# A recurrent attention with two dense layers: the order of all five engines taken from a list scheduler in the kernel's source

## The chip, the core and the metric

The kernel runs on one core of a Trainium2 chip. The core has five engines with a queue each: PE (TensorE) multiplies matrices, DVE (VectorE), ACT (ScalarE) and POOL (GpSimd) work element by element, and SP (SyncE) issues the DMA transfers. Each engine works through its own instructions in the order in which the program lists them, and semaphores hold an instruction back until its inputs are there. The metric is the device time of one execution in microseconds (us); the median of three runs stands for a kernel.

## The reference, cut to what matters

```python
batch, n_heads, seq, head_dim = 4, 8, 768, 40
for t in range(S):                                  # attention: a state per head, step by step
    y[:, :, t] = einsum('bhd,bhde->bhe', rt, state)
    Sa = einsum('bhde,bhe->bhd', state, at)
    state = state * wt - einsum('bhd,bhe->bhde', Sa, bt) + einsum('bhd,bhe->bhde', vt, kt)
x = y as (3072 tokens, 320)
h = x @ w_in                                        # layer one: 320 -> 2048 -> 320
x = (h * sigmoid(1.702 * h)) @ w_out
g, val = x @ w_gate, x @ w_val                      # layer two: 320 -> 1536 -> 320
out = (silu(g) * val) @ moe2_w_out
```

All weights arrive in 64 bits and are converted to 32 in the kernel.

## The kernel before, in words

The attention is worked out in chunks: 12 steps of 64 tokens (`T`, `NT`), all 32 heads at once. A step has two halves. The first half does not depend on the state. It loads the step's data (`load_w`, `load_a`, `load_kb`, `load_v`, `load_r`, `load_vt`, all issued by SP), forms the running products of the decays forward and backward (`scan`, `rec`, L371 and L386, on DVE), scales the keys with them (`scale_kb`, `scale_a`, L392 and L396), and multiplies keys by keys on PE (`g_nb`, L411 to L414, into the tile nb through ACT, L415; `g_nk`, L427). nb holds a triangular system. Its 32 by 32 blocks are inverted column by column in `solve`: DVE transposes nb to nsol (L448), 31 pivots follow, each a product (L462, tmp) and an addition (L467, tsol) that depend on each other, and a transposition gives tt (L471). The pivots of a step stand on fixed engines: the first 16 on DVE, the last 15 on POOL. Two small products (`g_q`, L487; `g_t`, L504) complete the inverse.

The second half carries the state mt from step to step: `g_w` (L523, L535), `g_u` (L558), `g_ut` (L575), `g_m` (L594), two score products `g_s` (L621), the result `g_y` (L639, L661) and the transposed state `g_mt` (L609). Its result goes by six small DMAs to the tile xm (`x_move`) and is split into a high and a low part in xst (`x_split`, L690 to L695), the input of layer one.

Layer one (`Up`) takes 512 tokens at a time, so two attention steps feed one of its six blocks m. For each of 16 slices f of the hidden layer, `h_part` issues 8 matmuls of 512 columns (L222), ACT applies Silu and copies the high part (L226, L228), POOL subtracts to get the low part (L230, gl), and `o_part` issues 8 matmuls two slices later (L244 to L253). The block of step pair (2m, 2m+1) can start when both steps are split. Layer two (`Down`) follows when layer one is done; it is not changed.

What sets the order around the change: in `layer_one` PE's order is the source's (`manual_schedule` with PE alone): 16 slots i a step, in each at most one or two attention products and then 8 matmuls of layer one, taken from the generator `dense`. Within a step, `g_w` stands in slot 0, `g_nb` of the next step in slot 1, `g_nk` and `g_y` in slot 8, `g_mt` in slot 9, `g_tok` in slots 10 and 11, `g_q` in slot 13, `g_t` in slot 15. The order of DVE, ACT, POOL and SP comes from the framework's scheduler, with priorities shifted by `later(att.tc, -200)` for pivots and `later(att.tc, 300)` for conversions. The weights' conversion (`Convert`, three operations on DVE, two on ACT and one on POOL for a piece, 89 pieces) is spread over the steps by `spread_out`: the 44 pieces of layer one over the first 3.5 steps, the 45 of layer two after them. The attention products share two PSUM tiles of two banks each; layer one's h product has one bank. nb, nsol, tsol, tt, q and kb exist once; a and c twice.

```python
engines = (nc.vector, nc.vector) if n == 0 else (nc.gpsimd, nc.vector)
init, work, end = att.solve(engines)
...
if i == 13 and ahead:
    att.g_q()
```

Of the kernel before, what the change touches and what calls it, by code (L numbers as in the profile page):

```python
# [20 lines left out]
T = 64  # L21
# [13 lines left out]
class later:  # L35
    def __init__(self, tc, off):
        self.tc, self.off = tc, off

    def __enter__(self):
        self.tc.cur_priority += self.off  # L40

    def __exit__(self, *a):
        self.tc.cur_priority -= self.off


# [12 lines left out]


TINY = 3.4332275390625e-05  # L60


class Convert:
# [4 lines left out]
    def __init__(self, tc, ctx):  # L68
        self.tc = tc
        self.nc = tc.nc  # L70
        self.p = ctx.enter_context(tc.tile_pool(name="cv", bufs=1))
        self.ps = Ring(ctx, tc, "cvs", 2)
        self.p2 = Ring(ctx, tc, "cv2", 2)
        self.p3 = Ring(ctx, tc, "cv3", 3)
        self.p1 = Ring(ctx, tc, "cv1", 1)

    def piece(self, src, finish):

        nc = self.nc
        st = {}  # L80
        wide = src.dtype != F32
        rows, cw = src.shape[0], src.shape[1] // (2 if wide else 1)

        def take():
            st["w"] = self.p2.tile([128, self.CW], F32, tag="cvw", name="cvw")

        def load():
            if wide:
                a = st["a"] = self.p3.tile([128, self.CW, 2], U32, tag="cva", name="cva")
                nc.sync.dma_start(out=a[0:rows, 0:cw].rearrange("p c k -> p (c k)"), in_=src)  # L90
            else:
                take()
                nc.sync.dma_start(out=st["w"][0:rows, 0:cw], in_=src)

        def square():
            take()
            lo, hi = (st["a"][0:rows, 0:cw, k] for k in range(2))
            nc.scalar.activation(out=st["w"][0:rows, 0:cw], in_=hi.bitcast(F32), func=ACTF.Square)  # L98

            nc.scalar.activation(out=lo, in_=lo, func=ACTF.Copy, scale=2.0 ** -29)  # L100

        def step(i):
            v = nc.vector
            lo, hi = (st["a"][0:rows, 0:cw, k] for k in range(2))
            if i == 0:
                st["u"] = self.p1.tile([128, self.CW], U32, tag="cvu", name="cvu")
            u, w = (st[n][0:rows, 0:cw] for n in "uw")
            f = u.bitcast(F32)
            if i == 0:
                v.tensor_scalar(  # L110
                    out=u, in0=hi, scalar1=3, scalar2=0x3FFFFFF8, op0=ALU.logical_shift_left, op1=ALU.bitwise_and
                )
            if i == 1:
                v.scalar_tensor_tensor(
                    out=u, in0=hi, scalar=0xC0000000, in1=u, op0=ALU.bitwise_and, op1=ALU.bitwise_or
                )
            if i == 2:
                v.scalar_tensor_tensor(out=f, in0=w, scalar=TINY * TINY, in1=f, op0=ALU.is_ge, op1=ALU.mult)  # L118
            if i == 3:
                nc.gpsimd.tensor_tensor(w.bitcast(U32), u, lo, op=ALU.add)  # L120

        steps = [square] + [lambda i=i: step(i) for i in range(4)] if wide else []
        return load, steps, lambda: finish(st["w"][0:rows, 0:cw])

    def split_out(self, w, view, *dst):

        nc = self.nc
        t = view(self.ps.tile([128, 512], F32R, tag="cvs", name="cvs"))
        hi, lo = t[:, 0], t[:, 1]
        w = w.rearrange("p (a c) -> p a c", c=hi.shape[2])  # L130
        nc.scalar.activation(out=hi, in_=w, func=ACTF.Copy)
        nc.gpsimd.tensor_tensor(lo, w, hi.bitcast(F32), op=ALU.subtract)
        n = hi.shape[1] // len(dst)
        for i, d in enumerate(dst):
            nc.sync.dma_start(out=d, in_=t[:, :, n * i:n * i + n].rearrange("p h a c -> p a h c").bitcast(F32))

    @staticmethod
    def chain(pieces):

        out = [pieces[0][0]] + [None] * 4  # L140
        finish = None
        for i, (_, steps, f) in enumerate(pieces):
            if finish and not steps:
                out.append(finish)
                finish = None
            if i + 1 < len(pieces):
                out.append(pieces[i + 1][0])
            out += steps[:3]
            if finish:
                out.append(finish)  # L150
            out += steps[3:]
            finish = f
        return out + [None, None, finish]


class Up:
# [9 lines left out]
    def __init__(self, tc, ctx, cst, w_out, x2s, side):  # L166
        self.nc, self.cst, self.w_out, self.x2s = tc.nc, cst, w_out, x2s
        pool = lambda name, bufs, **kw: Ring(ctx, tc, name, bufs, **kw)
        self.wp = pool("f_w", 1, side=side).pool
        self.xp = pool("f_x", 2, side=side)  # L170
        self.sp = pool("f_s", 3, side=side)
        self.gp = pool("f_g", 3, side=side)
        self.ph = pool("f_ph", 1, space=PSUM)
        self.pa = pool("f_pa", 1, space=PSUM)
# [99 lines left out]
    def steps(self):  # L274
# [12 lines left out]
        for x in lag:  # L287
            yield from self.o_part(*x)
# [1003 lines left out]
```

## Time and profile before

| | us |
|---|---|
| median of three runs | 1485.36 (1475.73 to 1490.98) |
| the profiled execution, device time | 1484.43 |
| its span, first to last instruction | 1482.6 |
| DVE busy, ACT busy, POOL busy | 658.5, 437.4, 393.9 |
| PE busy | 1161.4 |

The page of a profile gives busy times of engines, the chain of work that ended last, and the costliest groups of instructions. The views behind it ask the same execution for the busy time in stretches, for the instructions of one source line, for the engines' waits and for the instructions in order of time. A number such as x768 is a count; a name such as nsol<-nb reads "writes nsol, reads nb".

### The profile page before, as it was taken

To read this page: it belongs to the slowest core of one execution; us is meant where nothing else is said; L and a number is where in the kernel's file an instruction comes from. 1 tells how busy PE (TensorE), PEld (TensorE's weight loads), DVE (VectorE), ACT (ScalarE), POOL (GpSimd) and SP (SyncE) were. 2 spreads that over 40 slices of the span, in tenths; PEclk is the share of its full clock that TensorE was granted. 3 is DMA by queue.
4 is the path that set the end of the run, shared out by engine and by line. 5 is a ranking of instruction groups with operands and counts; after the bars stand their busy time and mean duration, and the time that the engine had idled before them with its cause. 6 is when DMAs were issued, how large, how long until landed. Compare 5 with 4: busy or idle time off the path is not lost.

```text
span 1482.6 us, 38220 instructions
## 1 busy us (share of the span) xinstructions
PE 1161.4 (78%) x16897; PEld 973.8 (66%) x16897; DVE 658.5 (44%) x1197; ACT 437.4 (30%) x830; POOL 393.9 (27%) x544
## 2 busy tenths in 40 slices
PE   1353449286877968687777788698999999999998
PEld 1353437265666857566666667586778888888887
DVE  5576575445645455525455463323433232323222
ACT  2123243233333223122323232324532222222221
POOL 3014453646444242414343443221000000000000
PEclk9975559678897879778988979799999999999999
DMA  6116151444525252323525252324620010100000
GB/s 153 49 55 190 50 165 56 135 119 119 148 87 153 71 164 85 120 80 109 149 67 144 67 159 77 111 63 160 214 63 22 19 39 1 39 1 19 1 18 20
DMA packets 71240, 131.99 MB, mean 89 GB/s; under 512 B 7128, under 2 KB 27608, under 8 KB 71064
## 3 DMA queue, kind: packets, MB, share of 16 engines
q1 hardware_dynamic: 71064, 129.45, 29.5%
q8 instruction: 134, 2.20, 0.6%
q14 instruction: 42, 0.34, 0.1%
HBM read 103.08 MB, written 19.79 MB: 83 GB/s over the span
## 4 chain that ended last, share of the span: by engine, by line
PE 50%; DVE 16%; POOL 12%; DMA 10%; issue 8%; ACT 2%; SPq 1%; POOLq 0%; DVEq 0%; ACTq 0%
PE gv L931 18%; PE h L222 6%; DVE tsol L467 4%; POOL tmp L462 4%; POOL tsol L467 4%; DVE tmp L462 3%; PE oacc L951 3%; PE oacc L952 3%; PE oacc L953 3%; POOL cvw L120 3%; DMA kb<-kba 3%; PE psw L535 2%; PE acc L249 2%; PE psw L523 2%; PE acc L251 2%
## 5 line engine op out<-in xcount | busy, mean ns | idle before, releaser
L931 PE MATMUL gv<-xst,wg 128*128 128x512 f32 x1152 | 281.5, 396 | 1.8 <-ACT sg L934 1.8
L931 PEld LDWEIGHTS gv<-xst,wg 128*128 128x128 f32 x1152 | 214.2, 188 | 48.7 <-ACT sg L934 2.3
L222 PE MATMUL h<-xst,wi 120*128 120x512 f32 x768 | 214.8, 423 | 18.8 <-ACT sg L226 15.6
L222 PEld LDWEIGHTS h<-xst,wi 120*128 120x128 f32 x768 | 148.1, 200 | 56.7 <-ACT sg L226 18.1
L230 POOL TENSOR_TENSOR gl<-sg,gh 128x512 fp32r<-128x512 f32 x82 | 117.4, 1432 | 222.7 <-ACT gh L228 210.9
L935 DVE TENSOR_TENSOR sg<-gv,sg 128x512 f32<-128x512 f32 x72 | 49.8, 691 | 230.0 <-PE gv L931 230.0
L120 POOL TENSOR_TENSOR cvw<-cvu,cva 128x256 uint32<-128x256 uint32 (+2 forms) x89 | 72.4, 814 | 175.0 <-DVE cvu L118 132.7
L249 PE MATMUL acc<-gh,wo 128*128 128x512 f32 x192 | 91.3, 476 | 5.8 <-DMA wo<-w_out 3.2
L609 PE MATMUL psd<-cst,mt 104*104 104x104 f32 x96 | 18.8, 375 | 91.0 <-DVE su L667 91.0
L952 PE MATMUL oacc<-wo,zh 128*128 128x320 f32 x288 | 88.9, 309 | 0.0
L951 PE MATMUL oacc<-wo,zh 128*128 128x320 f32 x288 | 88.8, 309 | 0.0
L953 PE MATMUL oacc<-wo,zl 128*128 128x320 f32 x288 | 88.3, 309 | 0.0
L934 ACT ACTIVATE sg<-gv 128x512 f32<-128x512 f32 x72 | 43.1, 599 | 151.0 <-PE gv L931 151.0
L427 PE MATMUL psk<-a,kb 40*64 40x64 f32 x768 | 22.6, 299 | 83.0 <-DVE su L624 62.6
L226 ACT ACTIVATE sg<-h 128x512 f32<-128x512 f32 x96 | 56.5, 588 | 97.9 <-PE h L222 92.3
L251 PE MATMUL acc<-gh,wo 128*128 128x512 f32 x192 | 84.0, 438 | 0.0
L253 PE MATMUL acc<-gl,wo 128*128 128x512 f32 x192 | 83.5, 436 | 0.0
L98 ACT ACTIVATE cvw<-cva 128x256 f32<-128x256 f32 (+2 forms) x89 | 38.1, 431 | 148.7 <-DMA w_gv<-cvw 83.7
L937 ACT ACTIVATE zh<-sg 128x512 fp32r<-128x512 f32 x72 | 45.5, 631 | 123.0 <-DVE sg L935 123.0
L110 DVE TENSOR_SCALAR cvu<-cva 128x256 uint32<-128x256 uint32 (+2 forms) x89 | 40.8, 459 | 90.3 <-POOL cvw L120 82.0
L609 PEld LDWEIGHTS psd<-cst,mt 104*104 104x104 f32 x96 | 14.9, 197 | 95.5 <-DVE su L667 95.4
L427 PEld LDWEIGHTS psk<-a,kb 40*64 40x64 f32 x768 | 20.4, 206 | 84.7 <-DVE su L624 63.7
(126 smaller groups left out, 2199.9 us busy)
## 6 DMA issues: line engine op xcount, KB each, us to landing
wo<-w_out SPq DMA_DIRECT2D x48, 640.0 KB
kb<-kba SPq DMA_DIRECT2D x24, 416.0 KB
cva<-out SPq DMA_DIRECT2D x35, 256.0 KB
cva<-gv SPq DMA_DIRECT2D x30, 256.0 KB
xm<-su SPq DMA_DIRECT2D x72, 80.0 KB
wdec<-wd SPq DMA_DIRECT2D x12, 422.9 KB
a<-kba SPq DMA_DIRECT2D x12, 416.0 KB
r<-rT SPq DMA_DIRECT2D x12, 416.0 KB
```

The source lines that it names most:

```text
L120: nc.gpsimd.tensor_tensor(w.bitcast(U32), u, lo, op=ALU.add)
L222: nc.tensor.matmul(ps, self.wi[:, b, 128 * f:128 * f + 128], x[:, a], start=(i == 0), stop=(i == 7))
L230: self.sub.tensor_tensor(lo, sg, hi.bitcast(F32), op=ALU.subtract)
L249: nc.tensor.matmul(acc[i], w[:, c:c + 128], hi, start=st, stop=False)
L251: nc.tensor.matmul(acc[i], w[:, 256 + c:384 + c], hi, start=False, stop=False)
L253: nc.tensor.matmul(acc[i], w[:, c:c + 128], lo, start=False, stop=sp)
L462: eng.tensor_tensor(tv, tsol[:, o:16, u:u + 1].to_broadcast([128, n, u]), nsol[:, u:u + 1, 0:u].to_broadcast([128, n, u]), op=ALU.mult,)
L467: eng.tensor_tensor(t, t, tv, op=ALU.add)
L931: nc.tensor.matmul(ps, w[:, b], x[:, a], start=(i == 0), stop=(i == 7))
L951: nc.tensor.matmul(acc[k], hi[:, c], self.wo[:, f, 0], start=st, stop=False)
L952: nc.tensor.matmul(acc[k], hi[:, c], self.wo[:, f, 1], start=False, stop=False)
L953: nc.tensor.matmul(acc[k], lo[:, c], self.wo[:, f, 0], start=False, stop=sp)
```

## The change

Every operation up to the end of the attention becomes a task with an engine (or a choice of engines), a cost in microseconds written in the source, the names it reads and writes, and a due value. `Plan.order` runs a list scheduler over all tasks while the kernel is built: it takes the task that can begin first and, among those of the same engine that can begin within 0.12 us of it, the one with the smallest due value. The resulting order is the program order of all five engines (`manual_schedule()` with no list of engines). A group of 8 matmuls of layer one is one PE task with the largest due value, so it goes where no attention product can begin. Tasks that may run on DVE or POOL are given to the one that would finish first: the pivots (product and addition of one pivot on one engine), the scaling of a and of both halves of kb, layer one's low part gl, and the low part in the split of xm. All copies of q and of tt out of PSUM go to ACT (half of them were on DVE). nb has two buffers. The two PSUM tiles are handed out by the plan. Tiles that rotated through rings become fixed tiles with the same numbers of buffers. `y_part(1)` no longer stands ahead of the rest of `g_y`, `g_m` stands ahead of `g_ut`, the last step leaves out `g_m`, and md is cleared once on POOL. Layer one's operations that the plan begins after the attention's last operation run after it under the framework's scheduler, as before, there with a second PSUM bank for h; four jobs of layer two's weights are issued after each PE task of it, instead of one after each matmul. The number of DMAs and their sizes stay, their order on SP is the plan's.

The diff, cut to its core:

```diff
+class Plan:
+    SEM, RATE, LATENCY, SLACK = 0.15, 215.0, 2.0, 0.12
...
+    def order(self):
+        free, ready, done = {}, {}, []
+        sets = [0.0] * self.sets
+        wire = 0.0
...
+        def start(t, e):
+            s = max(t.est[e], free.get(e, 0.0))
+            if t.bank and t.bank.slot is None:
+                if min(sets) >= 1e9:
+                    return None
+                s = max(s, min(sets))
+            mine = s + t.choice[e]
+            for o, c in t.choice.items():
+                if o != e and max(t.est[o], free.get(o, 0.0)) + c < mine - 1e-9:
+                    return None
+            return s
...
+            now, _, _, e, _ = min(found, key=lambda x: x[:3])
+            now, _, _, e, t = min((x for x in found if x[3] == e and x[0] <= now + self.SLACK),
+                                  key=lambda x: (x[1], x[2]))
...
+            if t.kb:
+                wire = max(wire, t.end) + t.kb / self.RATE
+                t.end = wire + self.LATENCY
...
 class Up:
...
+        def pe(cost, fn, reads, writes):
+            last[0] = add("PE", cost, fn, reads, writes, after=(last[0],))
+            last[0].due = 1e6
...
+            pe(1.95, mm, [f"x{m % 2}.{y}" for y in range(2)] + w, ("h",))
+            add("ACT", 0.6, silu, ("h",), (f"sg{s}",))
+            add("ACT", 0.63, lambda: nc.scalar.activation(out=hi, in_=sg, func=ACTF.Copy), (f"sg{s}",), (f"gh{d}",))
+            add(("POOL", "DVE"), (1.43, 0.69), lambda e: self.engine(e).tensor_tensor(lo, sg, hi.bitcast(F32), op=ALU.subtract),
+                (f"sg{s}", f"gh{d}"), (f"gl{d}",))
...
 class Attention:
...
-        self.nb = one.tile([128, 16, T], F32, name="nb")
+        self.nb = [one.tile([128, 16, T], F32, name=f"nb{i}") for i in range(2)]
...
+        nc.gpsimd.memset(self.md, 0.0)
...
+        plan.add("DVE", 2.4, scan, ("wdec",), (ck,), due + 0.1)
+        plan.add("DVE", 3.35, back, ("wdec",), ("rc",), due + 0.12)
+        plan.add(("POOL", "DVE"), (2.3, 1.7), scale_a, (ck,), (ak,), due + 0.13)
+        plan.add(("DVE", "POOL"), (1.7, 2.3), lambda e: scale(1, e), ("rc",), ("kb1",), due + 0.14)
...
+        plan.add("DVE", 2.0, turn, (nbk,), ("nsol",), due + 0.1)
+        for u in range(31, 0, -1):
+            x = (16 - u // 2) * u
+            both, cost = ("DVE", "POOL"), (0.2 + 0.0008 * x, 0.22 + 0.0019 * x)
+            t = plan.add(both, cost, lambda e, u=u: product(e, u), ("nsol", "tsol"), ("tmp",), due + 0.1)
+            plan.add(both, cost, lambda e, u=u: update(e, u), ("tmp",), ("tsol",), due + 0.1, same=t)
...
+        plan.add("PE", 1.15, q_mm, (nbk, "tt1"), ("q.p",), due + 0.84, bank=bq, into=("q0", "q1"))
+            plan.add(("ACT",), (0.75,), lambda e, p=p: move(e, bq, p, self.q), ("q.p",), (f"q{p}",), due + 0.85, bank=bq)
...
+        plan.add("PE", 2.4, w_mm, (ak, "mt", "nk", "v"), ("w.p",), due, bank=bw, into=("w",))
+        plan.add(("ACT",), (0.75,), w_out, ("w.p",), ("w",), due, bank=bw)
...
 def layer_one(att, up, conv, first, second):
...
+    dense = up.tasks(plan)
+    next(dense)
     for n in range(NT):
+        att.prepare(plan, n, n - 1.0)
+        if n == 1:
+            for q in range(4):
+                convert(first[q], 0.2 if q == 0 else 1.4 + 0.5 * q, 0.05)
+        if n > 3:
+            i = len(second) * (n - 4) // 8
+            convert(second[i:len(second) * (n - 3) // 8], n - 0.9, 0.15)
+        att.advance(plan, n, n)
+        if n % 2:
+            next(dense, None)
+    order = plan.order()
+    end = max(t.begin for t in order if not hasattr(t, "dense"))
+    with att.tc.manual_schedule():
+        for t in order:
+            if t.begin <= end:
+                t.run()
+    return [t for t in order if t.begin > end]
...
+                    up.tail = True
+                    for t in tail:
+                        t.run()
+                        if t.eng == "PE":
+                            down.prepare(4)
```

## Rows read from the trace of the kernel before

**Rows 1.** The page: its span, and the busy time of each engine.

```profile
span 1482.6 us, 38220 instructions
...
PE 1161.4 (78%) x16897; PEld 973.8 (66%) x16897; DVE 658.5 (44%) x1197; ACT 437.4 (30%) x830; POOL 393.9 (27%) x544
```

**Rows 2.** Busy us (instructions) of each engine by stage, granted PE clock, DMA share, GB/s.

```profile
0.00:1005.00 1005.00, 697.95 (x14604) 577.34 (x14605) 511.92 (x965) 297.54 (x580) 388.78 (x540) 0.81 0.37 109
1005.00:1077.00 72.00, 66.56 (x280) 52.89 (x279) 30.20 (x58) 37.62 (x78) 5.15 (x4) 0.98 0.58 188
1077.00:1470.00 393.00, 391.19 (x1980) 338.17 (x1979) 114.14 (x172) 100.85 (x171) 0.00 (x0) 1.00 0.07 21
...
0.00:144.00 144.00, 52.18 (x1548) 48.28 (x1552) 93.42 (x206) 34.89 (x71) 40.43 (x38) 0.82 0.41 113
```

**Rows 3.** Line L558: shortest, median, longest ns; its first and last start, us.

```profile
L558 PE MATMUL psu<-w,tt x768: 225/226/326, 76.3 to 977.7; 64*64 64x40 f32 x192
```

**Rows 4.** Chain of work that ended last, one step: start us, us, what.

```profile
570.26 1.13 PE psw L535 x32
...
576.03 1.04 ACT nb L415
577.09 1.99 DVE nsol L448
...
605.01 1.06 DVE tt L471
```

**Rows 5.** Instructions of PE in order of time, the same step: start us, us.

```profile
633.66 1.20 PE L487 MATMUL psq<-tt,nb 32*32 32x32 f32 x64
...
642.51 1.74 PE L504 MATMUL psx<-q,tn 32*32 32x32 f32 x62 [0.48 <-DVE q L494]
...
647.89 1.40 PE L523 MATMUL psw<-mt,a 40*64 40x40 f32 x22
```

**Rows 6.** Waits of all engines, 0 to 1003 us: us in total, times, longest.

```profile
DVE nsol L448 <- ACT nb L415: 118.0, 11, 18.4
...
DVE tt L471 <- POOL tsol L467: 80.3, 10, 11.8
```

**Rows 7.** Instructions of POOL and of DVE in order of time, around 556 us.

```profile
556.10 1.28 POOL L230 TENSOR_TENSOR gl<-sg,gh 128x512 fp32r<-128x512 f32 x1
```

**Rows 8.** The same of DVE.

```profile
556.14 2.32 DVE L392 TENSOR_TENSOR kb<-kb,rc 104x1024 f32<-104x1024 f32 x1 [5.95 <-DMA kb<-kba]
```

**Rows 9.** Single lines: count, shortest/median/longest ns, first and last start us.

```profile
L386 DVE TENSOR_TENSOR_SCAN rc<-wdec,rc x12: 2302/4029/4035, 9.6 to 871.2; 104x1040 f32<-104x1040 f32 x12
...
L392 DVE TENSOR_TENSOR kb<-kb,rc x12: 1215/1702/3007, 12.0 to 881.8; 104x1024 f32<-104x1024 f32 x12
...
L392 POOL TENSOR_TENSOR kb<-kb,rc x12: 2178/2198/3156, 13.9 to 879.3; 104x1024 f32<-104x1024 f32 x12
...
L230 POOL TENSOR_TENSOR gl<-sg,gh x82: 1260/1280/2859, 221.7 to 1024.1; 128x512 fp32r<-128x512 f32 x82
...
L230 DVE TENSOR_TENSOR gl<-sg,gh x14: 673/692/694, 1027.6 to 1073.3; 128x512 fp32r<-128x512 f32 x14
...
L462 DVE TENSOR_TENSOR tmp<-tsol,nsol x222: 178/264/1292, 35.3 to 912.3; 128x126 f32<-128x126 f32 x13, 128x31 f32<-128x31 f32 x11, 128x58 f32<-128x58 f32 x11, 128x81 f32<-128x81 f32 x11
L462 POOL TENSOR_TENSOR tmp<-tsol,nsol x150: 217/366/1217, 167.1 to 928.6; 128x135 f32<-128x135 f32 x10, 128x126 f32<-128x126 f32 x10, 128x130 f32<-128x130 f32 x10, 128x120 f32<-128x120 f32 x10
...
L118 DVE SCALAR_TENSOR_TENSOR cvu<-cvw,cvu x89: 353/425/1479, 23.1 to 992.7; 128x256 f32<-128x256 f32 x65, 120x256 f32<-120x256 f32 x16, 80x256 f32<-80x256 f32 x8
...
L120 POOL TENSOR_TENSOR cvw<-cvu,cva x89: 722/732/3402, 23.7 to 993.2; 128x256 uint32<-128x256 uint32 x65, 120x256 uint32<-120x256 uint32 x16, 80x256 uint32<-80x256 uint32 x8
```

**Rows 10.** Single lines of the first step and the copies, as in rows 9.

```profile
L411 PE MATMUL psn<-a,kb x768: 212/238/313, 15.1 to 900.0; 40*32 40x64 f32 x192
...
L448 DVE STREAM_TRANSPOSE nsol<-nb x12: 1901/1966/1985, 33.3 to 901.6; 128x1024 f32<-128x1024 f32 x12
...
L509 DVE COPY tt<-psx x12: 689/689/691, 65.9 to 966.8; 32x512 f32<-32x512 f32 x12
```

More of the change, by code (lines that the diff above doesn't have):

```diff
@@ new lines, in piece @@
+        self.count += 1
+        wk = f"cvw{i % 2}"
+        w = self.w[i % 2][0:rows, 0:cw]
+        if not wide:
+            load = lambda: nc.sync.dma_start(out=w, in_=src)
+            return [("SP", 0.5, load, (), (wk,), rows * cw / 256)] + finish(w)
+        ak = f"cva{i % 3}"
+        a = self.a[i % 3]
+        lo, hi = (a[0:rows, 0:cw, k] for k in range(2))
+        u = self.u[0:rows, 0:cw]
+        f = u.bitcast(F32)
+        def load():
+            nc.sync.dma_start(out=a[0:rows, 0:cw].rearrange("p c k -> p (c k)"), in_=src)
@@ L95, in square, with low @@
         def square():
-            take()
-            lo, hi = (st["a"][0:rows, 0:cw, k] for k in range(2))
-            nc.scalar.activation(out=st["w"][0:rows, 0:cw], in_=hi.bitcast(F32), func=ACTF.Square)
+            nc.scalar.activation(out=w, in_=hi.bitcast(F32), func=ACTF.Square)
+        def low():
             nc.scalar.activation(out=lo, in_=lo, func=ACTF.Copy, scale=2.0 ** -29)
[L102 to L120, printed above, removed]
@@ L137, in chain, with put @@
[L137 to L153, printed above, removed]
+        def put(j, d):
+            nc.sync.dma_start(out=d, in_=t[:, :, n * j:n * j + n].rearrange("p h a c -> p a h c").bitcast(F32))
@@ L199, in set_m, with copy @@
         hi, lo = self.wi[0:80, 4, c], self.wi[0:80, 5, c]
[L200 to L202 removed]
+        def copy(t):
             nc.sync.dma_start(
@@ L433, in g_tok @@
[L433 to L447 removed]
+        a, c, kb = self.a[n % 2], self.c[n % 2], self.kb
@@ new lines, in prepare @@
+        for p in range(2):
+            plan.add(("ACT",), (0.75,), lambda e, p=p: move(e, bt, p, tt[:, :, 32:64]), ("t.p",),
+                     ("tt0",) if p else ("tt0.0", "tt0"), due + 0.87, bank=bt)
+        plan.add(("POOL", "DVE"), (2.3, 1.7), lambda e: scale(0, e), ("rc",), ("kb0",), due + 0.3)
+        for k in range(2):
+            self.tokens(plan, k, due + 0.5 + 0.1 * k)
+        load(self.v.rearrange("q i d -> q (i d)"), self.vtok[n], "v", 328, 0.6)
+        load(self.r.rearrange("q p h t -> q (p h t)"), self.rT[n], "r", 416, 0.65)
@@ new lines, in give @@
+        k1 = tuple(f"xm1.{i}" for i in range(3, 6))
+        for i in range(4):
+            o = 2 * i if i < 2 else i + 2
+            keys = k0 if i < 2 else k1
+            f = (lambda e, i=i: low(e, i)) if i < 2 else (lambda e, o=o: mixed(o))
+            plan.add("ACT", 0.43, lambda o=o, i=i: high(o, i), keys, (f"xp{i}",), due, into=(key,))
+            es, cs = (("DVE", "POOL"), (0.62, 1.4)) if i < 2 else (("DVE",), (0.62,))
+            plan.add(es, cs, f, keys + (f"xp{i}",), (f"xq{i}",), due)
@@ L700, in bad_flag @@
+        plan.add("NONE", 0.001, lambda: None, tuple(f"xq{i}" for i in range(4)), (key,), due)
 def bad_flag(nc, tc, att, bad):
@@ new lines, in layer_one, with convert @@
+def layer_one(att, up, conv, first, second):
+    nc = att.nc
+    plan = Plan(2)
+    def convert(jobs, due, step):
+        for i, job in enumerate(jobs):
+            for eng, cost, fn, reads, writes, kb in job():
+                plan.add(eng, cost, fn, reads, writes, due + step * i, kb=kb)
+    dense = up.tasks(plan)
+    next(dense)
+    for n in range(NT):
+        att.prepare(plan, n, n - 1.0)
[15 more added lines that the diff above has]
+    return [t for t in order if t.begin > end]
```

1111 lines of the change are left out of this document (553 added, 558 removed).

## The prediction

> **What bounds the kernel now.** I read the page first. PE is busy for 1161.4 of 1482.6 us, but no engine is near full over the whole span [rows 1]. So I cut the span into stages [rows 2]. From 1077 to 1470 us layer two keeps PE busy for 391.2 of 393 us at full clock: that stage is PE's, and the change leaves it alone. From 1005 to 1077 us the last block of layer one runs, PE busy 66.6 of 72 us. The first 1005 us hold the attention and five of the six blocks. There PE is busy 698 us at a mean granted clock of 0.81, DVE 512, POOL 389, ACT 298: nobody is full. Something other than an engine's work sets that stage, and it holds two thirds of the time.
>
> The line of the u product shows the pace, since its 64 matmuls come once a step: the first at 76.3 us, the last step's at about 977.7 us [rows 3]. That is 901.4 us for 11 steps, 81.9 us each.
>
> The chain of waits shows what one step is made of [rows 4]. The w product of step 6 ends at 571.4, nb is out of PSUM at 577.1, nsol ready at 579.1, and the pivots run to 605.0, where tt starts. The inverse is needed next by psq on PE, which starts at 633.7 [rows 5]: 28 us after tt. The source puts psq in slot 13, behind the key products, y, the transposed state and the tokens, and PE works in that order whatever is ready. psx follows at 642.5 and the next w product at 647.9. So of 81 us, 26 are pivots, 28 are order, 14 the rest of the inverse, and the rest is w and nb. The waits say the same at the other end: DVE spends 118.0 us in 11 waits, 10.7 each, on nb, whose product stands behind the w product; and 80.3 us in ten waits on the POOL half of the pivots [rows 6].
>
> **The change part by part.** The sum is total = S + 11 x T + R, with S the start of the first u product, T the pace and R what follows the last one. Now it is 76.3 + 11 x 81.9 + 504.9 = 1482.6; the profiled device time is 1484.4, 1.8 more, and the median of the runs, 1485.4, is 0.9 above that.
>
> R, 504.9 us, is taken as unchanged. It holds the last 28 us of attention, block six, and layer two. Layer two's weight jobs now come 4 for a group of 8 matmuls instead of 8. There are 108, so they take 27 of the 32 groups. DVE and ACT, which do them, are busy 30 and 38 of those 72 us [rows 2], which hides it; without that cover at most the 5 last groups' worth, 5 x 72/32 = 11 us, would be late.
>
> S: the first key product starts at 15.1 us, nsol only at 33.3 [rows 10], while in the later step [rows 4] nsol starts 5.7 us after the w product's end. With 5 us from psn to nsol the inverse moves up by about 13 us, to S = 63; some of the order behind the pivots falls as well. I take 55, with 50 to 76 as bounds.
>
> T is the question. Three things bound it once the order is free.
>
> First the pivots. nsol, tsol and tt exist once, so a step cannot be shorter than its 62 dependent operations and a transposition: 26 us in rows 4. That is far below 81.9, so the ring of the inverse doesn't bind. The second nb belongs here: it lets the next nb be written while psq still reads the old one. Its cost is memory alone.
>
> Second PE. In 1005 us it has 698 us of work at clock 0.81 [rows 2]. If all of that shrinks with the clock it is 565 us at full clock. A step thus needs between 565/12 = 47 and 698/12 = 58 us, with layer one's groups (five blocks) in it.
>
> Third the pair of DVE and POOL, to which the change gives shared tasks. One case shows how it behaves: a gl on POOL from 556.10 to 557.38 [rows 7], and a key scaling on DVE that starts at 556.14 and takes 2.32 us [rows 8], where the shortest takes 1.22 [rows 9]: 1.10 longer, nearly all of gl's 1.28. The backward product takes 2.30 us at its shortest and 4.03 in the median. So two operations of these forms run one after the other even on two engines. The Trainium skill, page "SBUF — State Buffer", section "Who interferes with whom", says that a DVE instruction with two SBUF inputs and a GpSimd one that reads SBUF exclude each other and that the later one is blocked until the first ends. The row agrees. It speaks against sharing.
>
> I add up that work at undisturbed durations [rows 9]. Fixed: conversion on DVE 89 x 3 x 0.425 = 113, on POOL 89 x 0.73 and 44 split subtractions taken as equal, 97; two products of decays a step, 24 x 2.30 = 55. Shared: 744 pivot operations x 0.264 = 196 on DVE, x 0.366 = 272 on POOL; 80 gl x 0.69 = 55 or x 1.28 = 102; 36 scalings x 1.22 = 44 or x 2.20 = 79. All shared on DVE 265 + 295 = 560 us, all on POOL 265 + 453 = 718. A step is 47 to 60 us of exclusive work, 53 at half. The other end is that nothing of DVE and POOL overlaps and today's waits stay in: (511.9 + 388.8)/12 = 75 us. Transpositions and reads of PSUM on DVE are in the 75 and need not exclude POOL.
>
> I take T = 61. It is above the middle of the exclusive work, 53, because operations in a fixed order are late whenever one of another engine is, and above PE's 58 at today's clock; it is nearer to 53 than to 75 because the 75 counts blocked time twice. The gain of 20.9 us a step is less than the 28 + 10.7 us of order found above, so it has room there.
>
> The other edits cost little. Twenty-four copies leave DVE for ACT; at 0.69 us [rows 10] they free 17 us of DVE in all, and load ACT, busy 298 of 1005 us, by no more than about that. A POOL memset runs in the idle start. SP issues the same transfers in another order. A load there still waits in order, so one that waits for a pivot holds up the loads of weights and the six moves behind it, and scan and scaling wait for those. The same bytes in 760 instead of 1005 us need 144 GB/s; the tail moves 188 [rows 2].
>
> Sum: 55 + 11 x 61 + 504.9 = 1230.9, with 1.8 for device time 1232.7: **1233 us**, 0.83 of before.
>
> **The rivals.** *The exclusion decides.* By that rule of "SBUF — State Buffer" every shared task on POOL costs DVE its time. As a mechanism of this kernel: the plan counts the engines as free side by side, the chip lines the operations up, and every busy microsecond of the two adds. Then T = 75: 55 + 825 + 504.9 + 1.8 = 1387 us. For it: 2.32 us instead of 1.22. Against it: the pair already has 900.7 us in 1005, and some of that overlaps.
>
> *PE becomes the bound.* Until the first block is ready at about 55 + 61 + 28 = 144 us, PE has little to do; in the kernel before it was busy for 52 us by then, which leaves 646 [rows 2]. At today's clock and 95% busy that takes 680 us and ends the stage at 144 + 680 = 824, where I have 55 + 671 + 28 = 754: 70 us more, 1303 us. At full clock, 646 x 0.81 / 0.95 = 551, it would end at 695 and not bind. My number therefore wants the clock above 0.81, for which a PE with fewer gaps speaks: with PE busy 66.6 of 72 us it is 0.98 [rows 2].
>
> *The plan is met.* Shared tasks mostly on DVE, T = 48: 55 + 528 + 506.7 = 1090 us.
>
> *Slower.* The fixed order brings the waits back: the plan's nb or pivot is late because its operation was blocked, DVE waits for it in order with the conversions and the scans queued behind, PE waits for those, and the 10.7 us a step on nb remain. T = 75 + 10.7 = 86: 55 + 946 + 506.7 = 1508 us. It decides from T = (1482.6 - 504.9 - 55)/11 = 83.9 on.
>
> *The order changes nothing.* Another chain of about 82 us a step stands behind the present one, and time stays within 1%. The ring of 26 us speaks against it.
>
> **How the numbers follow.** Forecast 0.46, PE 0.15, exclusion 0.20, plan met 0.06, no change 0.04, slower 0.09. The forecast's own range is T from 53 to 69: 1145 to 1321. The whole range reaches from 1140 over PE's 1303 to just past the exclusion's 1387, 1395, and leaves out 0.19. A measurement here tells about 1% from no change. Faster by over 1% has 0.46 + 0.15 + 0.20 + 0.06 = 0.87, of which I move 0.01 to slower for cases between 1387 and 1508: 0.86, 0.04, 0.10.
>
> **What would show it.** Right: u products 55 to 67 us apart; psq within some 5 us of tt; the wait for nb far below 118 us; POOL busy not above 389 us and DVE carrying more pivots than 222; granted clock before layer two above 0.81; layer two still 393 us. Wrong: u products 75 us apart with pivots of over 1 us, which is the exclusion; PE busy in every tenth with layer one's groups left over after the attention, which is PE; DVE waiting in new places for PE or SP.

## The result and the profile after

The changed kernel takes 1317.27 us (median of 4, 1309.81 to 1321.51) beside 1488.17 for the kernel before in the same comparison: a ratio of 0.8855, 95% interval 0.8783 to 0.8927. The forecast was 1233, its range 1140 to 1395. The profiled execution takes 1321.51 us, 1.8 more than its span. One of the two executions of pool_extra_set below (1336 us) ran in a slower state, at a granted clock of 0.88 for 0.90, and is left out.

The page of the changed kernel, its span, busy times and two of its lines in 40 slices of 33 us:

```profile
span 1319.7 us, 38084 instructions
...
PE 1127.1 (85%) x16761; PEld 963.8 (73%) x16761; DVE 682.7 (52%) x1189; ACT 450.6 (34%) x853; POOL 358.4 (27%) x527
...
PE   2666884768688898897999999897999999999997
...
PEclk9966785875768989797989999998999999999999
```

Busy time by stage, which answers to [rows 2] (window, length, busy us with instructions of PE, PE's weight loads, DVE, ACT and POOL, granted clock, DMA share, GB/s): to 144 us, to the last u product, to the first product of layer two, the stretch between these two, and layer two:

```profile
0.00:144.00 144.00, 81.95 (x2692) 76.08 (x2692) 108.20 (x206) 41.24 (x80) 59.52 (x86) 0.79 0.41 116
...
0.00:725.00 725.00, 555.34 (x13722) 478.68 (x13726) 510.63 (x919) 272.35 (x539) 356.32 (x525) 0.82 0.48 137
...
0.00:915.40 915.40, 729.53 (x14745) 619.46 (x14745) 566.78 (x1016) 348.75 (x681) 358.37 (x527) 0.85 0.46 135
724.70:915.40 190.70, 174.50 (x1051) 141.08 (x1047) 56.15 (x97) 76.40 (x142) 2.05 (x2) 0.98 0.40 129
915.40:1308.00 392.60, 392.59 (x1984) 339.64 (x1985) 113.85 (x171) 100.44 (x170) 0.00 (x0) 0.99 0.06 19
```

The u product's line, which answers to [rows 3]:

```profile
L737 PE MATMUL ps<-w,tt x768: 226/226/326, 50.8 to 724.7; 64*64 64x40 f32 x192
```

So S is 50.8, T is (724.7 - 50.8)/11 = 61.3, and R is 1319.7 - 724.7 = 595.0. The forecast had 55, 61 and 504.9. Two terms of the sum came out as said; the third is 90.1 us longer. Layer two itself is not: 392.6 us, as before. What grew lies between the last u product and layer two: 190.7 us where it was 1076.9 - 977.7 = 99.2. Layer one's matmuls in that stretch, counted by the tiles h and acc of the changed kernel (PE first, its instructions in parentheses):

```profile
724.70:915.40 190.70, 89.38 (x352) 65.85 (x352) 26.08 (x44) 0.98 0.40 129
...
724.70:915.40 190.70, 92.64 (x368) 70.03 (x368) 4.11 (x6) 3.55 (x6) 0.98 0.40 129
```

That is 720 matmuls, 90 of the 192 groups of 8. The same count in the kernel before gives 168 and 184, 44 groups:

```profile
977.70:1076.90 99.20, 43.86 (x168) 0.98 0.48 157
...
977.70:1076.90 99.20, 46.30 (x184) 0.98 0.48 157
```

The 46 more, at 190.7/90 = 2.12 us each, are 97 us.

The waits of the first 752 us (total, times, longest), which answer to [rows 6]:

```profile
DVE su L836 <- PE ps L828: 48.9, 12, 6.6
...
DVE gl L365 <- ACT gh L364: 48.7, 24, 7.5
...
DVE nsol L571 <- ACT nb L478: 19.5, 7, 4.2
...
DVE tt L600 <- POOL tsol L588: 12.3, 5, 4.2
```

The two waits of before are nearly gone (118.0 and 80.3 us); in their place DVE waits for y's product and for ACT's high part, some 4 and 2 us a time. PE takes psq when tt is there. One step in order of time, DVE's line and then PE's:

```profile
470.79 1.05 DVE L600 STREAM_TRANSPOSE tt<-tsol 128x512 f32<-128x512 f32 x1 [2.17 <-POOL tsol L588]
...
474.72 1.51 PE L621 MATMUL ps<-tt,nb 32*32 32x32 f32 x43
```

Here psq starts 2.9 us after tt's end, the longest of the twelve gaps, seven of which are 0.2 us or less; in [rows 4, 5] it was 28 us from tt's start.

The pivots, however, now take longer. In this step nsol begins at 415.12 and the next one at 475.44:

```profile
415.12 1.97 DVE L571 STREAM_TRANSPOSE nsol<-nb 128x1024 f32<-128x1024 f32 x1 [3.55 <-ACT nb L478]
...
475.44 1.88 DVE L571 STREAM_TRANSPOSE nsol<-nb 128x1024 f32<-128x1024 f32 x1
```

From nsol's end at 417.1 to tt's start at 470.8 are 54 us, where [rows 4] has 26. Over the last eleven steps these stretches are 31 to 57 us long, 43 in the mean, against 26 in the kernel before. The pivots' own operations take some 25 us a step of it (303.9 us on both engines over twelve steps); the rest passes between them, with other work on the two engines. And since nsol and tsol exist once, the next nsol cannot begin before the pivots are done: in four of the eleven turns it begins less than 4 us after tt's end.

### The profile page after: what moved, and what is told of

It is laid out like the page before. It is cut to its first block, busy times and chain, and to the rows that moved or that the text cites. A ratio compares the mean times of both kernels' runs of the same rounds, so it can differ in the third digit from the quotient of the medians.

```text
span 1319.7 us, 38084 instructions
## 1 busy us (share of the span) xinstructions
PE 1127.1 (85%) x16761; PEld 963.8 (73%) x16761; DVE 682.7 (52%) x1189; ACT 450.6 (34%) x853; POOL 358.4 (27%) x527
## 5 line engine op out<-in xcount | busy, mean ns | idle before, releaser
L351 PE MATMUL h<-xst,wi 120*128 120x512 f32 x768 | 210.5, 418 | 9.8 <-ACT sg L359 4.8
L365 DVE TENSOR_TENSOR gl<-sg,gh 128x512 fp32r<-128x512 f32 x87 | 64.7, 744 | 125.4 <-ACT gh L364 125.3
L580 POOL TENSOR_TENSOR tmp<-tsol,nsol 128x30 f32<-128x30 f32 (+20 forms) x175 | 86.2, 492 | 75.8 <-DVE tsol L588 38.6
L580 DVE TENSOR_TENSOR tmp<-tsol,nsol 128x120 f32<-128x120 f32 (+20 forms) x197 | 74.5, 378 | 25.1 <-POOL tsol L588 19.1
L588 POOL TENSOR_TENSOR tsol<-tsol,tmp 128x30 f32<-128x30 f32 (+20 forms) x175 | 81.5, 466 | 11.7
L382 PE MATMUL acc<-gh,wo 128*128 128x512 f32 x192 | 82.7, 431 | 0.0
L383 PE MATMUL acc<-gh,wo 128*128 128x512 f32 x192 | 79.1, 412 | 0.0
L384 PE MATMUL acc<-gl,wo 128*128 128x512 f32 x192 | 77.7, 404 | 0.0
L1056 DVE TENSOR_TENSOR zl<-sg,zh 128x512 fp32r<-128x512 f32 x72 | 49.8, 692 | 43.7 <-ACT zh L1054 43.3
L557 PE MATMUL ps<-a,kb 40*32 40x64 f32 x768 | 29.1, 274 | 48.1 <-POOL kb L530 23.8
L588 DVE TENSOR_TENSOR tsol<-tsol,tmp 128x120 f32<-128x120 f32 (+20 forms) x197 | 61.7, 313 | 6.2
```

The costliest lines, as they stand in the source:

```text
L351: nc.tensor.matmul(ps[:, 0:n], self.wi[:, b, 128 * f:128 * f + 128], x[:, a], start=(e == 0), stop=(e == 7))
L365: add(("POOL", "DVE"), (1.43, 0.69), lambda e: self.engine(e).tensor_tensor(lo, sg, hi.bitcast(F32), op=ALU.subtract), (f"sg{s}", f"gh{d}" ...
L382: nc.tensor.matmul(acc[k], w[:, c:c + 128], hi, start=st, stop=False)
L383: nc.tensor.matmul(acc[k], w[:, 256 + c:384 + c], hi, start=False, stop=False)
L384: nc.tensor.matmul(acc[k], w[:, c:c + 128], lo, start=False, stop=sp)
L580: self.engine(e).tensor_tensor(tv, tsol[:, o:16, u:u + 1].to_broadcast([128, m, u]), nsol[:, u:u + 1, 0:u].to_broadcast([128, m, u]), op=A ...
```

## The experiments

The table holds what all runs showed. Groups left are those of layer one after the last u product; PE's busy and idle time are those up to layer two's first product (S, T and R in us, as above). These columns are read from the profiled execution (weights_early's took 1284 us); the time is the median, and each ratio is to the kernel before as it was timed beside that run (1479 to 1488 us).

| run | S | T | groups left | R | layer two starts | PE busy | PE idle | time | ratio to before |
|---|---|---|---|---|---|---|---|---|---|
| before | 76.3 | 81.9 | 44 | 504.9 | 1076.9 | 764 | 312 | 1485 | 1 |
| changed | 50.8 | 61.3 | 90 | 595.0 | 915.4 | 730 | 186 | 1317 | 0.8855 |
| fixed_engines | 51.6 | 62.1 | 90 | 592.7 | 922.2 | 741 | 181 | 1332 | 0.8996 |
| all_on_dve | 50.4 | 69.8 | 44 | 509.0 | 922.6 | 722 | 201 | 1329 | 0.8981 |
| weights_early | 53.7 | 59.1 | 82 | 578.5 | 877.1 | 718 | 159 | 1275 | 0.8609 |
| short_h | 51.3 | 59.5 | 90 | 544.7 | 845.6 | 619 | 227 | 1250 | 0.8431 |
| plan_for_pe_only | 91.5 | 74.4 | 90 | 590.9 | 1096.7 | 756 | 341 | 1505 | 1.0135 |
| one_nb | 51.5 | 62.9 | 88 | 587.6 | 925.8 | 731 | 195 | 1334 | 0.8987 |
| plan_with_port | 50.1 | 67.3 | 59 | 534.3 | 921.0 | 728 | 193 | 1329 | 0.8955 |
| port_and_early | 52.2 | 67.1 | 45 | 509.6 | 894.5 | 707 | 188 | 1301 | 0.8773 |
| pool_extra_sub | 54.1 | 64.4 | 86 | 585.4 | 944.1 | 738 | 207 | 1349 | 0.9091 |
| pool_extra_set | 51.5 | 61.6 | 86 | 584.1 | 909.2 | 727 | 182 | 1315 | - |
| pe_costs_early | 54.9 | 59.3 | 103 | 625.9 | 928.9 | 732 | 197 | 1332 | 0.8972 |
| groups_cheap_early | 53.5 | 62.0 | 60 | 537.6 | 869.3 | 709 | 161 | 1275 | 0.8599 |

The ratios' 95% intervals reach 0.004 (groups_cheap_early) to 0.007 (the changed kernel) to either side; for pool_extra_set, whose time is that of a single execution, none is given.

The theory was that the free order is the gain, that DVE and POOL, which exclude each other, set T, and that R grew because PE has too little to do early and is left with layer one's groups at the end. The rivals: PE's work or clock sets T too; the sharing or the second nb is the gain; the order of PE alone would do.

**short_h: does PE's work set T?**

```diff
-for e, (a, b) in enumerate(self.PAIRS):
+for e, (a, b) in enumerate(self.PAIRS[0:1] + self.PAIRS[7:8]):
```

> Same order on all engines; the h groups of layer one issue 2 of their 8 matmuls (the others, corrections and two of three row blocks, are left out, so h is not the reference's). That takes 96 x 6 matmuls off PE, at 0.23 us each 132 us at full clock. Theory A (T is set by DVE and POOL; PE's work sets only what is left over behind the attention): T stays 57 to 62, and the left-over shrinks so that layer two's first product follows the last split by some 45 us: 835 to 850 instead of 915, time 1230 to 1255. Rival (PE sets the pace too): T falls in proportion to PE's work, to 53 or below, time below 1180.

Measured: T 59.5, R 544.7, layer two from 845.6 on, time 1250. With 576 matmuls gone T moves by 1.8 us and R by 50; all three numbers of the theory came out, and the rival's T of 53 did not. PE's work does not set T by itself; it sets how long the left-over takes (90 groups as before, in 139.5 us instead of 190.7). PE's busy time falls by 111 us only, at a lower granted clock:

```profile
0.00:845.60 845.60, 618.66 (x14170) 523.59 (x14170) 569.63 (x1016) 345.91 (x681) 357.03 (x527) 0.80 0.50 146
```

That is 0.80 where the changed kernel had 0.85 up to layer two.

**all_on_dve and fixed_engines: what does the sharing bring?** The first gives every shared task to DVE, as in the line below; the second fixes the engines as in the kernel before.

```diff
-both, cost = ("DVE", "POOL"), (0.2 + 0.0008 * x, 0.22 + 0.0019 * x)
+both, cost = ("DVE",), (0.2 + 0.0008 * x,)
```

> The plan stays, but every task that DVE and POOL may share is given to DVE; POOL keeps only the conversions' addition and the split subtractions. Theory A (exclusion: work on POOL costs DVE its time anyway, and is slower there): pivots return to their short durations (mean product near 267 ns), T 58 to 66, time 1295 to 1350. Rival (the two engines do work side by side): the plan counts 58.0 us a step here against 45.2; by the stretch of 1.35 that is 78 us a step, 1500 us; without stretch on one engine 58, but then layer one's groups are the same backlog.

> The plan stays, the sharing is undone: the pivots below the sixteenth, gl, a and the first half of kb go to POOL, the rest to DVE, as in the kernel before; the order is the plan's for these engines. Theory A (the free order is the gain; DVE and POOL exclude each other, so what one takes over the other loses): u products 59 to 64 us apart, time 1300 to 1335, within about 1% of the changed kernel's 1317. Rival (the sharing is a part of the gain: engines side by side): the plan's own sum for this version ends layer one 21 us later, stretched as the chip stretched the plan (60.9 us a step for 45.2, times 1.35) 29 us: 1346 or more.

All on DVE, the pivots are undisturbed (their products and additions, mean ns behind the busy time; the changed kernel's first):

```profile
L580 DVE TENSOR_TENSOR tmp<-tsol,nsol 128x120 f32<-128x120 f32 (+20 forms) x197 | 74.5, 378 | 25.1 <-POOL tsol L588 19.1
L588 DVE TENSOR_TENSOR tsol<-tsol,tmp 128x120 f32<-128x120 f32 (+20 forms) x197 | 61.7, 313 | 6.2
```

```profile
L588 DVE TENSOR_TENSOR tsol<-tsol,tmp 128x126 f32<-128x126 f32 (+22 forms) x372 | 99.0, 266 | 11.9
L580 DVE TENSOR_TENSOR tmp<-tsol,nsol 128x126 f32<-128x126 f32 (+22 forms) x372 | 97.6, 262 | 11.6
```

Yet T is 69.8, above the theory's range (58 to 66) and below the rival's 78. The pivots of a step are back to 28 us in the mean, so it is not they that make it. Two other things can: DVE carries POOL's share, and the plan, which counts on slower steps, put 46 more groups of layer one ahead of the last u product. In groups_cheap_early below 22 more groups moved that product by 32 us; at that rate 46 groups would be 67 of the 94 us that eleven steps took longer, an estimate. The run does not part the two. The time is 1329, within the theory's range, because R is 86 us shorter, 509.0. With fixed engines T is 62.1 and the time 1332, as the theory had it. The choice of engine task by task is worth 1 to 2% of the time.

**weights_early: why is so much left over?**

```diff
-convert(first[q], 0.2 if q == 0 else 1.4 + 0.5 * q, 0.05)
+convert(first[q], -0.9 + 0.3 * q, 0.05)
```

> One number changes: the due values of layer one's weight conversions, -0.9 + 0.3 q for 1.4 + 0.5 q, so the plan puts the 44 pieces into the first 210 us instead of 280. Theory A (R grew by 90 us because PE stands idle for want of converted weights from 140 to 405 us, and these groups are left over behind the attention): block 0 ends by about 320 instead of 405, the first layer-two product comes 20 to 60 us earlier than 915, time 1255 to 1300. Rival 1 (PE's clock or work bounds, not the weights' date): no gain over 1%, 1305 to 1330. Rival 2 (DVE is full, so earlier conversions push pivots back by the same time): the first steps are later by 40 us or more and the end with them, 1317 to 1360.

The 44 pieces of layer one's weights are under way by 246 us, where the changed kernel had begun 26 by 245. PE (first number behind the length) in two stretches, the changed kernel's rows and then this kernel's:

```profile
150.00:250.00 100.00, 67.54 (x2052) 58.95 (x2052) 76.64 (x113) 38.60 (x79) 67.30 (x88) 0.79 0.45 131
250.00:400.00 150.00, 115.04 (x2543) 100.41 (x2546) 96.36 (x159) 55.80 (x118) 96.17 (x149) 0.71 0.47 134
```

```profile
150.00:250.00 100.00, 80.57 (x1508) 65.90 (x1499) 78.81 (x135) 48.97 (x106) 66.80 (x100) 0.79 0.52 151
250.00:400.00 150.00, 129.36 (x3355) 109.38 (x3354) 93.81 (x138) 57.41 (x104) 86.10 (x138) 0.89 0.47 137
```

PE's idle time in these 250 us falls from 67 to 40 us, and the clock in the second stretch rises from 0.71 to 0.89. Block 0 ends at 316 us instead of 424 (the first copy of its result), layer two begins 38 us earlier, and 1275 us is 3% below the changed kernel. The theory's forecast holds, neither rival's does, and the late weights are shown as a cause of a part: 82 groups are still left over.

**plan_for_pe_only: is the order of all five engines needed?**

```diff
-with att.tc.manual_schedule():
+with att.tc.manual_schedule(engines={nc.tensor.engine}):
```

> The plan's order holds for PE alone; DVE, ACT, POOL and SP get their order from the framework's scheduler as in the kernel before (with two nb buffers and the plan's choice of engines kept). Theory A (the 28 us a step behind tt and the nb product behind the w product were PE's order, so PE's order is the gain): T 58 to 70; and since layer one's left-over on PE takes up what a longer T gives, time 1300 to 1345. Rival (the order of all five engines is needed: PE's fixed order then waits for operations which the scheduler put late): T above 72, time above 1365.

1505 us, a ratio of 1.0135 (1.0081 to 1.0189): the whole gain is gone, and the time is about 1% above the kernel before. My theory was wrong here and the rival right (T 74.4). The scheduler, which no longer has the `later` hints of the kernel before, takes the conversions first: DVE's line of their first operation has run 57 times by 210 us, where the changed kernel has 18 (count, shortest, median and longest ns, first and last start):

```profile
L204 DVE TENSOR_SCALAR cvu<-cva x57: 242/293/1127, 17.8 to 209.9; 128x256 uint32<-128x256 uint32 x33, 120x256 uint32<-120x256 uint32 x16, 80x256 uint32<-80x256 uint32 x8
```

And of PE's waits, psq's for tt:

```profile
PE ps L621 <- DVE tt L600: 54.8, 2, 42.1
```

The pivots come behind them, S is 91.5, and PE stands up to 42.1 us at psq, whose place its order fixes. Nor is it the start alone: from step three (u copied at 305 us) to step twelve (at 910) a step still takes 67 us. Not tested is PE's order from the plan with such hints for the other engines.

**one_nb: the second buffer**

```diff
-self.nb = [one.tile([128, 16, T], F32, name=f"nb{i}") for i in range(2)]
+self.nb = [one.tile([128, 16, T], F32, name="nb")] * 2
```

> One nb buffer, all else the plan's. Theory A (the second buffer shortens a step by little, and the left-over of layer one on PE takes up the difference, as it did when T went from 61 to 69.5): T 61 to 65, R smaller by as much as 11 T grows, time 1305 to 1335. Rival (the second buffer is what removed the wait for nb, 118 us before): the wait comes back with 5 us a step or more and the time is 1350 or above.

T is 62.9 and the time 1334, at the upper end of the theory's range. DVE's wait for nb is 28.1 us in nine waits, against 19.5 with two buffers and 118.0 before:

```profile
DVE nsol L571 <- ACT nb L478: 28.1, 9, 5.4
```

So the order removed it, not the buffer. The buffer gives 1.6 us a step and a little over 1% of the time. The left-over took up less of it than the theory said: eleven steps are 18 us longer, R is 7 us shorter.

**pool_extra_sub and its twin pool_extra_set: the exclusion by itself**

```diff
+def extra():
+    nc.gpsimd.tensor_tensor(self.bal[:, 800:1280], self.bal[:, 0:480], self.bal[:, 0:480], op=ALU.subtract)
+for t in marks:    # behind the pivots 26, 21, 16, 11, 6
+    plan.add("POOL", 1.3, extra, (), ("bal",), due + 0.1, after=(t,))
```

The twin has `nc.gpsimd.memset(self.bal, 0.0)` in `extra`.

> Sixty operations that nobody needs are added to POOL, five among the pivots of each step: a subtraction of 480 columns with SBUF inputs, about 1.2 us each by the 1.28 us of the 512 column one, 6 us a step in time that POOL has free. Plan and order are those of its twin, pool_extra_set. Theory A (POOL's reading operations and DVE's with two SBUF inputs exclude each other): DVE's pivots are blocked, T is 2 to 6 us above the twin's, and DVE's product at least 15% longer in the mean. Rival (POOL and DVE run side by side): T within 1 us of the twin. In both theories PE's left-over takes up most of a longer T, so the time stays between 1310 and 1350.

> The twin: the same sixty places and the same plan, but each extra operation is a memset of 1280 columns on POOL, about as long (1024 columns took 0.95 us), without an input. Theory A (what excludes is POOL's reading): T 60 to 63 as in the changed kernel (60.9), DVE's product as there (378 ns in the mean) or shorter. Rival (any work of POOL blocks, or only POOL's occupation delays its own pivots): T and the products as in pool_extra_sub.

DVE's pivots and POOL's extra operations (busy us, mean ns, idle time before them), with the subtraction and then with the memset:

```profile
L582 DVE TENSOR_TENSOR tmp<-tsol,nsol 128x133 f32<-128x133 f32 (+17 forms) x215 | 86.8, 404 | 38.1 <-POOL tsol L590 31.4
L590 DVE TENSOR_TENSOR tsol<-tsol,tmp 128x133 f32<-128x133 f32 (+17 forms) x215 | 81.4, 379 | 6.6
...
L605 POOL TENSOR_TENSOR bal<-bal 128x480 f32<-128x480 f32 x60 | 62.7, 1045 | 1.9
```

```profile
L582 DVE TENSOR_TENSOR tmp<-tsol,nsol 128x133 f32<-128x133 f32 (+17 forms) x215 | 72.9, 339 | 35.1 <-POOL tsol L590 28.4
L590 DVE TENSOR_TENSOR tsol<-tsol,tmp 128x133 f32<-128x133 f32 (+17 forms) x215 | 61.4, 286 | 6.6
...
L605 POOL MEMSET bal<- 128x1280 f32 x60 | 69.9, 1165 | 1.4
```

With the same plan and the same counts, and although the memset is the longer, the subtraction makes DVE's products 19% and its additions 33% longer and T 64.4 instead of 61.6. POOL's reading blocks DVE: 5.2 us of it in a step cost 2.8 (the theory said 2 to 6). One part of both expectations failed: the left-over did not take up the longer T. The times are 1349 and 1315, and layer two starts 35 us later, for the 31 us that eleven steps took longer. Both kernels have 86 groups left, since the number is fixed when the order is made; the chip does not move a group.

**plan_with_port and port_and_early: a plan that knows the exclusion.** The list scheduler treats DVE's operations, except those that read PSUM or transpose, and all of POOL's as one resource. The costs of many operations become undisturbed ones (2.35 for 3.35 us for the backward product, 1.3 for 1.43 for a gl on POOL), so two things change at once.

```diff
+if e in ("DVE", "POOL") and not t.free:
+    free["PORT"] = t.end
```

> The list scheduler counts DVE's operations with two SBUF inputs and all of POOL's as one shared resource, with their undisturbed durations as costs. Its own sum: u products 57.5 us apart, layer one done at 809 us (738 in the plan of the changed kernel, which the chip stretched by 1.35 a step). Theory A (the exclusion makes the stretch): the chip now keeps the plan: T 57 to 62, pivots near their short durations, layer one done by 860 to 905, time 1260 to 1310. Rival (the stretch comes from waits of a fixed order for PE, DMA and others): stretched again by 1.2 to 1.35, T 69 to 78, time 1330 to 1420.

> The plan with the shared resource, and the early due values of layer one's weights (as in weights_early, 1275). Its own sum: first u at 47, last at 685, layer one done at 790. Theory A (exclusion makes the stretch, and the early weights fill PE from 160 us on): T 57 to 63, layer one done by 830 to 865, time 1225 to 1265. Rival (PE is full from 250 us on in weights_early, so a better fitting plan has nothing left to give): 1265 to 1300.

DVE's products in plan_with_port are undisturbed again:

```profile
L586 DVE TENSOR_TENSOR tmp<-tsol,nsol 128x126 f32<-128x126 f32 (+19 forms) x294 | 79.7, 271 | 9.8 <-POOL tsol L594 0.7
```

But T is 67.3, 1.17 times the plan's 57.5, and the times are 1329 and 1301. The theory said 57 to 62 and shorter times, the rival 69 to 78; neither holds for T, and both times lie at the edge of the rivals' ranges. A step is stretched also where no pivot is blocked. Whether T is longer than 61.3 because the plan keeps the two engines apart is not shown: it also puts 31 more groups ahead of the last u product, which at the rate of groups_cheap_early would be 45 of the 66 us that this product comes later, an estimate.

**pe_costs_early and groups_cheap_early: how many groups to put in.** Both start from weights_early and change costs in the plan alone. The first raises PE's costs to those of the trace; the second lowers a layer-one group's:

```diff
-pe(1.95, mm, ...)
+pe(1.4, mm, ...)
```

> Early weights as in weights_early (1275), and the plan's costs of PE's operations are those which the trace of the changed kernel shows (nb 4.1 for 2.1, w 4.0 for 2.4, y 3.8 for 3.0, a layer-one group 2.15 for 1.95, the rest by 0.05 to 0.6 more). The plan then has PE full from 200 us on and layer one done at 851 instead of 722. Theory A (PE's busy time and its idle time up to layer two make the end, and the order loses PE time because the plan thinks PE has room): idle PE time before layer two falls from 159 to below 145, layer two begins by 865, time 1235 to 1265. Rival (PE's idle time is set by the first 150 us and by waits that no cost tells): 1265 to 1300.

> weights_early (1275) with one more number changed: the plan counts a layer-one group on PE at 1.4 us for 1.95. It then puts 132 of the 192 groups ahead of the last u product instead of 110, which leaves 60 instead of 82. Theory A (over all runs R, what follows the last u, is 505 us at 44 groups left and grows by 2 us for each further group; PE has 112 us without work in the attention stage, which the 22 groups can fill): R falls from 578 to about 537; T grows by less than the groups' 46 us, to 58.7 to 61, and the time is 1235 to 1262. Rival (the groups delay attention's products by as much as they take: PE waits in order, so a fuller order shifts everything): last u later by 40 us or more, time 1265 to 1295.

With the higher costs the plan sees no room for groups: 103 are left, R is 625.9 and the time 1332, above what either theory said. T was 59.3, as in weights_early, though 21 fewer groups stood ahead of the last u product. With the lower cost 60 are left (h and acc):

```profile
735.70:869.30 133.60, 59.88 (x232) 44.21 (x232) 17.62 (x30) 0.96 0.45 140
...
735.70:869.30 133.60, 61.11 (x248) 46.63 (x248) 2.74 (x4) 2.37 (x4) 0.96 0.45 140
```

R is 537.6, where 537 was forecast, but the last u product comes 32 us later (T is 62.0, above the theory's 61), and 1275 us (ratio 0.8599, 0.8563 to 0.8635) is no better than weights_early's 1275 (0.8609, 0.8560 to 0.8658). PE's idle time stayed at 161 us: the groups pushed attention's products back instead of filling gaps. The rival was right on the time.

## Why the prediction was right, and where it was wrong

**The chain.** Right: psq follows tt at once, the wait for nb fell from 118.0 to 19.5 us and that for the POOL pivots from 80.3 to 12.3.

**S.** Right: 50.8 for 55; the first nsol starts at 17.3 us instead of 33.3, 16 us earlier where 13 were forecast.

**T.** The number is right, 61.3 for 61; its reasons are only partly, so some of it is luck. That it would lie above PE's 58 says little, as PE's work turned out not to set it by itself (short_h). The exclusion is real and has a price (the twins), and the rival's T of 75 was not reached. But the lower bound of exclusive work, 47 us with all shared tasks on DVE, was tried in that form and took 69.8. And "so the ring of the inverse doesn't bind" was read from 26 us of pivots in the old order. In the new one they take 43 us in the mean, and in four of eleven turns the ring does bind. Shorter pivots alone do not shorten the step, though (28 us in all_on_dve). What fills the rest of a step is not settled: the plan's steps were stretched by 1.17 with the pivots undisturbed and by 1.35 in the changed kernel.

**R.** This is the step that failed: "R, 504.9 us, is taken as unchanged." It held block six and little else only because PE had nearly finished five blocks when the attention ended. By the prediction's own numbers, steps of 61 us left PE 610 us (144 to 754) for 646 us of work. To fit that at 95% busy the clock would have had to be 646 x 0.81 / 0.95 / 610 = 0.90; the text asked only for more than 0.81. Granted were 0.82 up to the last u product and 0.85 up to layer two, so that sign was met and told nothing.

What the runs showed in its place: 90 groups of layer one are left instead of 44, and R is 595.0. Want of room was not all of it. Between 144 and 724.7 us PE was busy for 729.5 - 82.0 - 174.5 = 473 of 581 us, so it stood idle for 108 us with 90 groups to come. How many groups stand ahead of the attention's end is fixed when the order is made: with less work on PE it is still 90 left (short_h), with other costs in the plan 60 or 103. And over the thirteen kernels that leave the groups whole, R follows from their number: 505 to 510 at 44 or 45, 534 and 538 at 59 and 60, 579 at 82, 584 and 585 at 86, 588 at 88, 591 to 595 at 90, 626 at 103. That is (625.9 - 504.9)/(103 - 44) = 2.05 us for a group, so 46 groups more are 94 us at that rate, and 90.1 were measured.

**The rival that was nearest** is "PE becomes the bound" (1303 us, chance 0.15), but its time came close by two errors that nearly cancel. Its 646 us are five blocks' work; with block six, 66.6 us, it asks PE for 712 us after 144 us and has layer two begin at 824 + 72 = 896. Measured up to layer two at 915.4 are 729.5 - 82.0 = 647.5 us, 65 less: 30 more were done before 144 us (82 for 52), and PE's whole busy time up to layer two was 35 shorter. Its fill was lower too: 647.5 in 771.4 us is 84%, 124 us idle, where the rival had about 95% and 40 us. The late weights account for 27 us of PE's idle time (weights_early); the rest is open.

**What the gain is.** Up to layer two PE is busy and idle for 764 + 312 us before and 730 + 186 after. The row of before:

```profile
0.00:1076.90 1076.90, 764.42 (x14882) 0.82 0.39 114
```

Of 161 us gained, 126 were idle time of PE and 35 are busy time, for nearly the same matmuls (14745 and 14882 records) at a granted clock of 0.85 instead of 0.82. The 26 + 227 us that S and T gave are 253; 90 of them went back into R. The free order is what is left of the gain's causes when the sharing (fixed_engines) and the second nb (one_nb) have been taken away; the smaller edits, such as the copies moved to ACT or `g_m` ahead of `g_ut`, were not tested one by one.

**The range.** It held in part by luck. 1317 lies at the end of the forecast's own 1145 to 1321, but that range was made for T up to 69, and T was 61: the miss was in R, which had no range. The whole range, 1140 to 1395, took it in because the PE rival stood in it.

**The other signs.** POOL 358.4 us, not above 389: right. DVE carrying more pivots than 222: wrong, it carries 197. Layer two 392.6 us: right; whether 32 groups would have covered its weight jobs was not tested, as more were left. Granted clock above 0.81: right, and too weak a sign, as said. DVE waiting in new places: it does, in waits of a few us. PE busy in every tenth with groups left over, the sign for PE: the groups are there, but none of the first fourteen slices in the page's line is a 9.

**The second nb** was taken as a buffer that lets the next nb be written early. It does, for 1.6 us a step.

## What to carry to other kernels

When a stage is shortened, add up the work that other engines do in its shade before calling what follows it unchanged: here the forecast had 646 us of matmuls for 610 us, at 0.81 of the clock, and still took R as it was. With a fixed order, the amount of filler left at the end is decided by the plan's costs when the order is made, and moving it earlier helps only as far as it fills idle time; so look for what lets the filler start sooner (the weights' conversion here, 3%). A chain that is short in one order need not be so in the next: the pivots went from 26 to 43 us in the new one. And the order planned for all engines lost its whole gain when it was kept for PE alone, without hints for the others.

## What the runs showed of the hardware

Work of about the same length on POOL costs DVE more when POOL reads: with sixty subtractions of 1.05 us added DVE's products took 404 ns in the mean, with sixty memsets of 1.17 us in the same places 339. The Trainium skill, page "SBUF — State Buffer", section "Who interferes with whom", says that a DVE instruction with two SBUF inputs contends with a GpSimd one that reads SBUF and not with one that only writes; the twins agree, T 64.4 against 61.6.

PE's time for the same 14745 or 14746 matmuls up to layer two ran from 707 us (port_and_early, granted clock 0.87) to 756 (plan_for_pe_only, 0.82). The one with the lower clock is the one in which PE was idle longer, 341 us against 188. First port_and_early's row up to layer two, then plan_for_pe_only's:

```profile
0.00:894.50 894.50, 706.84 (x14745) 601.60 (x14746) 597.33 (x1266) 351.61 (x681) 199.48 (x277) 0.87 0.47 138
```

```profile
0.00:1096.70 1096.70, 756.14 (x14745) 640.59 (x14745) 538.13 (x1016) 359.15 (x681) 311.71 (x527) 0.82 0.38 113
```
